# First expert layer as seven products of quarters, read from PSUM between products and interleaved with the second layer

## Chip, cores, metric

The kernel runs on one NeuronCore of a Trainium2 chip. The metric is device time in microseconds (us), the median of several executions. The engines are TensorE (PE in the profile; its weight loads are listed apart as PEld), VectorE (DVE), ScalarE (ACT), GpSimd (POOL) and SyncE (SP). A "call" below is one batch of runs measured together on one chip.

## The reference

An attention block makes a matrix `x` of 4608 tokens by 512; then eight experts, each of two layers, are summed with weights `P` that are balanced by eight rounds of row and column normalisation.

```python
def _moe_ref(x, w_gate, w1, w2):                # x 4608x512, w1 8x512x1024, w2 8x1024x512
    P = exp(logits - max)                       # logits = x @ w_gate, 8 experts
    for _ in range(8):                          # the balancing
        P /= P.sum(1, keepdims=True) + 1e-09
        P /= P.sum(0, keepdims=True) + 1e-09
        P *= N / E
    for e in range(E):
        h = np.maximum(x @ w1[e], 0.0)          # first layer
        out += P[:, e:e+1] * (h @ w2[e])        # second layer
```

## The kernel before

All matmul operands are fp16. `xT` holds x transposed (128 partitions, 4 blocks of the 512 inputs, 4608 tokens). A chunk is 512 tokens. For each chunk the first layer makes 8 hidden tiles of 4 matmuls each, ScalarE applies the relu on the way from PSUM to SBUF, and the second layer makes 4 output tiles of 8 matmuls each, which VectorE scales and adds into `acc`.

```python
def ffn1(hT, w, j, fts=range(FT)):              # FT = 8 hidden tiles
    for ft in fts:
        h_ps = ps_h[ft % len(ps_h)].tile([P, TCH], FP32, name="h_ps")
        for kt in range(KT):                    # KT = 4
            te.matmul(out=h_ps[:], lhsT=w[0][:, kt, ft*P:(ft+1)*P],
                      rhs=xT[:, kt, j*TCH:(j+1)*TCH], start=(kt == 0), stop=(kt == KT-1))
        se.activation(out=hT[:, ft, :], in_=h_ps[:], func=AF.Relu)

def ffn2(hT, e, w, j, ts, y_ps=None, fts=range(FT)):
    # ... 8 matmuls of 512 columns into y_ps, then:
    ve.scalar_tensor_tensor(out=acc(g), in0=y_ps[:], scalar=P_tok[:, g, e:e+1], in1=acc(g),
                            op0=ALU.mult, op1=ALU.add)
    # ... the last expert's rows are stored from here

# attention interleaved with expert 0 on tokens that are ready (cut), then:
for it in range(8): ...                          # balancing: VectorE, with two tiny matmuls a round
for j in range(B, NJ): ffn(0, w0, j)             # rest of expert 0
for g in range(NG): nc.gpsimd.tensor_scalar(...) # acc *= P[:, 0]
for e in range(1, E):
    w = w_next; ...                              # load the next expert's weights
    for j in range(NJ): ffn(e, w, j)
```

The softmax here doesn't subtract the row's maximum and nothing guards it: scores larger than these inputs give would overflow.

## Time and profile before

| before | value | where it stands |
|---|---|---|
| median time | 1101.5 us | runs |
| PE busy | 1074.0 of 1099.8 us | page, part 1 |
| experts 1 to 7, both layers | about 124 us each | 576 matmuls x 215.8 ns |
| PE idle in 185 to 245 us (end of expert 0) | 1.77 us | table by stage, 60.00 - 58.23 |

First the page of the kernel before: the busy times of the engines with instruction counts, and the chain of work that ended last, by engine.

```profile
PE 1074.0 (98%) x6064; PEld 500.9 (46%) x6064; DVE 353.5 (32%) x642; ACT 425.7 (39%) x782; POOL 124.8 (11%) x160
...
PE 92%; DVE 5%; issue 1%; ACT 1%; POOL 1%; DMA 1%; DVEq 0%; POOLq 0%
```

The chain of waits runs through PE for 92% of the span, so PE time is what counts. The groups of instructions (line, engine, operation, output and inputs, count; then busy us, mean ns of one; then idle time before them and what ended it) show where it goes:

```profile
L137 PE MATMUL y_ps<-w2e,hT 128*128 128x512 f16 x2048 | 453.7, 379 | 0.7 <-DVE acc_lo L152 0.7
L122 PE MATMUL h_ps<-xT,w1e 128*128 128x512 f16 x2048 | 454.0, 379 | 0.0
L152 DVE SCALAR_TENSOR_TENSOR acc_lo<-y_ps,P_tok,acc_lo 128x512 f32<-128x512 f32 x224 | 168.3, 751 | 598.4 <-PE y_ps L137 594.3
```

A matmul record lasts 379 ns, but 2048 of them keep PE busy for 454 us, that is 222 ns each: records of consecutive matmuls overlap. The timeline (start, length, engine, operation, count) gives the pitch directly.

```profile
399.66 3.62 PE L137 MATMUL y_ps<-w2e,hT 128*128 128x512 f16 x16
...
400.72 0.75 DVE L152 SCALAR_TENSOR_TENSOR acc_lo<-y_ps,P_tok,acc_lo 128x512 f32<-128x512 f32 x1 [0.98 <-PE y_ps L137]
```

Sixteen matmuls take 3.62 us; without the last one's 0.379 that is 15 pitches of 216 ns. VectorE starts its accumulation at 400.72 while PE goes on. The table by stage (stretch in us, its length, then busy us and count for PE, PEld, DVE, ACT and POOL, then granted clock, DMA share, GB/s) shows the state of the kernel before in its last part:

```profile
185.00:245.00 60.00, 58.23 (x300) 25.72 (x300) 28.70 (x61) 22.87 (x41) 14.28 (x11) 1.00 0.38 61
...
300.00:500.00 200.00, 200.00 (x928) 90.67 (x927) 44.31 (x59) 67.78 (x114) 3.33 (x4) 1.00 0.13 22
```

From 245 us on PE is busy all the time and VectorE is used for 22% (44.31 of 200), ScalarE for 34%. Both have room for extra work, if PE gets less.

### The profile page before, as it was taken

The numbers are of one execution on the slowest core, as the hardware profiler recorded it, in microseconds if no ns is written. First come the engines' busy times: TensorE is split into PE (matmuls) and PEld (weight loads), VectorE is DVE, ScalarE is ACT, GpSimd is POOL, SyncE is SP. The second block draws the span as 40 slices with busy tenths as digits, with TensorE's granted clock in tenths as the row PEclk, the third lists the DMA queues.
The fourth block names the chain that finished last, engine by engine and source line by source line (L and its number), as shares of the span: only waits on it lengthen the run. The fifth ranks groups of instructions, "written<-read, shape, count | busy, mean of one in ns | idle before, by whom it ended". The sixth has DMA issues, their size and how long they took to land.

```text
span 1099.8 us, 14392 instructions
## 1 busy us (share of the span) xinstructions
PE 1074.0 (98%) x6064; PEld 500.9 (46%) x6064; DVE 353.5 (32%) x642; ACT 425.7 (39%) x782; POOL 124.8 (11%) x160
## 2 busy tenths in 40 slices
PE   4899999999999999999999999999999999999998
PEld 3455555444444444444444444444444444444443
DVE  6787775542222222222222222222222222222222
ACT  3666665333333333333333333333333333333332
POOL 7532200059400000000000000000000000000000
PEclk9999999999999999999999999999999999999999
DMA  9965404220004000040004000040004000013333
GB/s 166 195 90 83 66 1 75 42 40 1 1 1 76 1 1 1 1 77 1 1 1 70 8 1 0 1 77 1 1 1 64 14 1 1 1 39 77 77 78 77
DMA packets 34353, 41.32 MB, mean 38 GB/s; under 512 B 3568, under 2 KB 26096, under 8 KB 34288
## 3 DMA queue, kind: packets, MB, share of 16 engines
q0 software_dynamic: 28000, 30.94, 18.2%
q1 hardware_dynamic: 6288, 9.46, 3.8%
q8 instruction: 47, 0.77, 0.3%
q14 instruction: 18, 0.15, 0.0%
HBM read 61.88 MB, written 9.44 MB: 65 GB/s over the span
## 4 chain that ended last, share of the span: by engine, by line
PE 92%; DVE 5%; issue 1%; ACT 1%; POOL 1%; DMA 1%; DVEq 0%; POOLq 0%
PE y_ps L137 40%; PE h_ps L122 39%; PE y_ps L88 5%; PE small_ps L88 4%; PE h_ps L88 4%; DVE k_p L88 1%; DMA k_ld<-in_k_dram 1%; DVE q_p L88 1%; DVE colp L513 0%; DVE v_aug L88 0%; DVE q_pT L88 0%; DVE den L88 0%; DVE P_tok L508 0%; DVE P_tok L523 0%; PE small_ps L519 0%
## 5 line engine op out<-in xcount | busy, mean ns | idle before, releaser
L129 ACT ACTIVATE hT<-h_ps 128x512 f16<-128x512 f32 x512 | 305.7, 597 | 574.7 <-PE h_ps L122 574.7
L137 PE MATMUL y_ps<-w2e,hT 128*128 128x512 f16 x2048 | 453.7, 379 | 0.7 <-DVE acc_lo L152 0.7
L122 PE MATMUL h_ps<-xT,w1e 128*128 128x512 f16 x2048 | 454.0, 379 | 0.0
L152 DVE SCALAR_TENSOR_TENSOR acc_lo<-y_ps,P_tok,acc_lo 128x512 f32<-128x512 f32 x224 | 168.3, 751 | 598.4 <-PE y_ps L137 594.3
L137 PEld LDWEIGHTS <-hT 128*128 128x128 f16 x2048 | 199.9, 98 | 241.2 <-issue 1.0
L122 PEld LDWEIGHTS <-w1e 128*128 128x128 f16 x2048 | 199.7, 98 | 239.7
L103 POOL DMA_DIRECT2D w1e<-in_moe_w_dram x11 | 8.3, 758 | 603.8 <-PE h_ps L122 551.7
L88 PE MATMUL h_ps<-xT,w1e 128*128 128x512 f16 x256 | 65.7, 383 | 0.0
L88 PE MATMUL y_ps<-w2e,hT 128*128 128x512 f16 x256 | 61.4, 380 | 0.0
L542 POOL TENSOR_SCALAR acc_lo<-acc_lo,P_tok 128x512 f32<-128x512 f32 x32 | 49.3, 1556 | 10.1 <-DVE P_tok L523 10.1
L88 ACT ACTIVATE hT<-h_ps 128x512 f16<-128x512 f32 x64 | 38.4, 600 | 21.8 <-PE h_ps L88 21.4
L152 DVE SCALAR_TENSOR_TENSOR acc_hi<-y_ps,P_tok,acc_hi 128x512 f32<-128x512 f32 x28 | 21.0, 751 | 75.7 <-PE y_ps L137 75.7
L88 PE MATMUL small_ps<-ident,q_p 128*128 128x128 f16 x288 | 27.7, 231 | 13.2 <-DVE q_p L88 9.5
L88 PEld LDWEIGHTS <-hT 128*128 128x128 f16 x256 | 22.7, 98 | 29.6 <-issue 6.2
L88 PEld LDWEIGHTS <-q_p 128*128 128x128 f16 x288 | 20.5, 103 | 25.2 <-DVE q_p L88 12.0
L88 ACT COPY rb<-small_ps 128x384 f32<-128x384 f32 x64 | 22.4, 402 | 24.4 <-PE small_ps L88 24.4
L88 DVE TENSOR_TENSOR xT<-small_ps,rb 128x384 f16<-128x384 f32 x64 | 26.3, 453 | 16.9 <-ACT rb L88 15.7
L88 PEld LDWEIGHTS <-w1e 128*128 128x128 f16 x256 | 22.2, 98 | 18.3 <-issue 1.7
L88 DVE TENSOR_SCALAR q_pT<-small_ps 128x384 f16<-128x384 f32 x48 | 26.1, 552 | 6.1 <-PE small_ps L88 5.5
L88 DVE TENSOR_TENSOR k_p<-k_ld,acc_hi 128x1152 f16<-128x1152 f16 x32 | 24.0, 751 | 5.7 <-ACT k_ld L88 5.7
L88 ACT ACTIVATE k_ld<-k_ld 128x576 f16<-128x576 f16 x32 | 22.1, 690 | 6.3 <-DMA k_ld<-in_k_dram 6.3
L88 ACT ACTIVATE q_pT<-small_ps 128x384 f16<-128x384 f32 x48 | 23.6, 497 | 2.3 <-PE small_ps L88 2.3
(80 smaller groups left out, 289.5 us busy)
## 6 DMA issues: line engine op xcount, KB each, us to landing
out_dram<-acc_lo SPq DMA_DIRECT2D x64, 128.0 KB, 2.3
w1e<-in_moe_w_dram POOLq DMA_DIRECT2D x7, 1024.0 KB, 8.2
w2e<-in_moe_w_dram POOLq DMA_DIRECT2D x7, 1024.0 KB, 9.0
q_ld<-in_q_dram POOLq DMA_DIRECT2D x32, 144.0 KB, 4.8
k_ld<-in_k_dram POOLq DMA_DIRECT2D x32, 144.0 KB, 4.6
v_ld<-in_v_dram POOLq DMA_DIRECT2D x32, 144.0 KB, 4.9
w1e<-in_moe_w_dram POOLq DMA_DIRECT2D x4, 256.0 KB, 7.0
w2e<-in_moe_w_dram POOLq DMA_DIRECT2D x4, 256.0 KB, 6.9
```

The source lines that it names most:

```text
L88: return tc.keep_in_program_order(getattr(self.engine, name)(*args, **kwargs))
L103: nc.gpsimd.dma_start(out=w[0][:, :, f0:f1], in_=view[:, :, f0:f1])
L122: te.matmul(out=h_ps[:], lhsT=w[0][:, kt, ft * P : (ft + 1) * P], rhs=xT[:, kt, j * TCH : (j + 1) * TCH], start=(kt == 0), stop=(kt == KT ...
L129: se.activation(out=hT[:, ft, :], in_=h_ps[:], func=AF.Relu)
L137: te.matmul(out=y_ps[:], lhsT=hT[:, ft, ts * P : (ts + 1) * P], rhs=w[1][:, ft, :], start=(ft == 0), stop=(ft == FT - 1),)
L152: ve.scalar_tensor_tensor(out=acc(g), in0=y_ps[:], scalar=P_tok[:, g, e : e + 1], in1=acc(g), op0=ALU.mult, op1=ALU.add,)
L542: nc.gpsimd.tensor_scalar(out=acc(g), in0=acc(g), scalar1=P_tok[:, g, 0:1], scalar2=None, op0=ALU.mult,)
```

## The change

The intent: the first layer of experts 1 to 7 is a matrix product, tokens by hidden units. It is cut into halves of tokens, of inputs and of hidden units, and the eight products of quarters are replaced by seven (Strassen's method in Winograd's form). That takes 7/8 of the columns through PE, and needs sums of quarters of x (once, `S1`, `S2`, `S4`, and one over `a21`), sums of quarters of each expert's weights (`T1` to `T4`), and sums of products. In the code `b11` to `b22` are the quarters of the expert's weights, and `Y` and `Z` are further PSUM banks beside `X`. For the sums of products, partial sums are used twice: a PSUM bank `X` accumulates four products, and ScalarE copies it ("snapshots" `u1`, `u2`, `u4`) between them. PE may write the bank again only after each copy, so second-layer matmuls of the unit before are put in between ("fillers", 4 matmuls each). A unit is 2 x 384 tokens, and has 4 groups; expert 1's first unit carries the end of the balancing in its fillers.

```diff
+    def group(hT, tw, n, i, filler):
+        X = ps_h[0].tile(...); Y = ps_s.tile(...)
+        product(X, b11, x_part(0, 0, n), True)        # each product: 2 matmuls of 384 columns
+        u1 = snapshot(X, "u1")                        # ScalarE copy to fp16
+        product(Y, b21, x_part(0, 1, n), True)
+        add_relu(h11, Y, u1)                          # VectorE: add from PSUM, then max with 0
+        for fn in late: fn()                          # last product of the group before
+        filler()                                      # 4 matmuls of the second layer
+        product(X, T2, s_part(S2, n), False)
+        u2 = snapshot(X, "u2")
+        product(Z, T3, x_part(1, 0, n), True)
+        filler()
+        product(X, T1, s_part(S1, n), False)
+        u4 = snapshot(X, "u4")
+        add_relu(h22, Z, u4)
+        filler()
+        product(X, b22, s_part(S4, n), False)
+        nc.scalar.activation(out=h12, in_=X[:, 0:TU], func=AF.Relu)
+        def last():
+            product(Z, T4, x_part(1, 1, n), False)
+            add_relu(h21, Z, u2)
+        late.append(last)
 ...
-    for e in range(1, E):
-        for j in range(NJ):
-            ffn(e, w, j)
+    for e in range(1, E):
+        for n in range(NU):                           # 6 units
+            if e == 1 and n == 0: ... tws[i] = w_sums(w, i)       # sums of weights
+            if e == 1 and n + 2 < NU: for _ in x_sums(n + 2): pass # sums of x
+            for i in range(FH):                       # 4 groups
+                group(hT, tws[i], n, i, fill)
+                ...                                   # weight sums for the next expert
+            pending = halves(...)                     # this unit's second layer, in fillers of the next
```

Four more parts came with it. PE's instructions are now in written order for the whole kernel (before, a scheduler placed them after the attention). The balancing is spread over the end of expert 0 and the first unit of expert 1. The tile `hA`, expert 0's hidden tile of the attention part, now shares memory with what follows. The very last store is issued by ScalarE. A few buffer counts changed with it (`hB` from 3 to 2, the small PSUM tiles from 2 to 4).

Copying a bank in the middle of its accumulation rests on what the Trainium skill says in "PSUM — Partial Sum Buffer", "The four PSUM rules": only the first-matmul flag clears anything, and a matmul without it adds to what the bank holds; the last-matmul flag has no effect.

More of the change, by code (lines that the diff above doesn't have):

```diff
@@ L59 @@
     wA = ctx.enter_context(tc.tile_pool(name="wA", bufs=1))
-    hA = ctx.enter_context(tc.tile_pool(name="hA", bufs=1))
     sk_pool = ctx.enter_context(tc.tile_pool(name="sk_pool", bufs=2))
@@ L84, in __init__ @@
             self.engine = engine
+            self.last = None
         def __getattr__(self, name):
             def call(*args, **kwargs):
-                return tc.keep_in_program_order(getattr(self.engine, name)(*args, **kwargs))
+                i = getattr(self.engine, name)(*args, **kwargs)
+                if self.last is not None:
+                    tc.add_manual_dep(
+                        i.ins,
+                        self.last.ins.name,
+                        mybir.DependencyInfo(
+                            mybir.DependencyClass.NoSync, mybir.DependencyReason.DATA
+                        ),
+                        reason="written order",
+                    )
+                self.last = i
+                return i
             return call
@@ L128, in ffn1, with ffn2 @@
                 )
-            se.activation(out=hT[:, ft, :], in_=h_ps[:], func=AF.Relu)
-    def ffn2(hT, e, w, j, ts, y_ps=None, fts=range(FT)):
-        g = j * TCH // P + ts
+            se.activation(out=hT[:, ft, 0:TCH], in_=h_ps[:], func=AF.Relu)
+    def ffn2(hT, e, w, c0, g, y_ps=None, fts=range(FT)):
         if y_ps is None:
@@ L138, in ffn2 @@
                 out=y_ps[:],
-                lhsT=hT[:, ft, ts * P : (ts + 1) * P],
+                lhsT=hT[:, ft, c0 : c0 + P],
                 rhs=w[1][:, ft, :],
@@ L160, in ffn2 @@
                     rows = out[b * S : (b + 1) * S].rearrange("(p c) d -> p c d", c=C)
-                    nc.sync.dma_start(
+                    (nc.scalar if half and g == NG - 1 else nc.sync).dma_start(
                         out=rows[:, c, :], in_=acc(g)[half * HP : (half + 1) * HP, :]
@@ L165 @@
     with ExitStack() as p1:
+        hA = p1.enter_context(tc.tile_pool(name="hA", bufs=1))
         cs_pool = p1.enter_context(tc.tile_pool(name="cs_pool", bufs=1))
@@ L483 @@
                     at(j, NS - 1, turn, b + 1, hk, k_)
-        for j in range(B):
+        for j in range(B - 1):
             hT = hA.tile([P, FT, TCH], F16, name="hT")
@@ L492 @@
                         y_ps = ps_y.tile([P, Dm], FP32, name="y_ps")
-                    ffn2(hT, 0, w0, j, ts, y_ps, range(part * FT // 2, (part + 1) * FT // 2))
+                    ffn2(
+                        hT, 0, w0, ts * P, j * TCH // P + ts, y_ps,
+                        range(part * FT // 2, (part + 1) * FT // 2),
+                    )
                 for fn, args in todo.get((j, slot), []):
                     fn(*args)
-    te, ve, se = free
-    ps_h.append(ctx.enter_context(tc.tile_pool(name="ps_h2", bufs=2, space=bass.MemoryType.PSUM)))
@@ L500 @@
-    ps_s = ctx.enter_context(tc.tile_pool(name="ps_k", bufs=2, space=bass.MemoryType.PSUM))
-    for it in range(8):
-        rs = sk_pool.tile([P, NG], FP32, name="rs")
-        nc.vector.reduce_sum(out=rs[:], in_=P_tok[:], axis=AX.X)
-        rr = sk_pool.tile([P, NG], FP32, name="rr")
-        nc.vector.reciprocal(out=rr[:], in_=rs[:])
-        nc.vector.tensor_tensor(
-            out=P_tok[:], in0=P_tok[:],
-            in1=rr[:].unsqueeze(2).to_broadcast([P, NG, E]), op=ALU.mult,
-        )
-        colp = sk_pool.tile([P, E], FP32, name="colp")
-        nc.vector.reduce_sum(out=colp[:], in_=P_tok[:].rearrange("p c e -> p e c"), axis=AX.X)
-        tot_ps = ps_s.tile([P, 512], FP32, name="small_ps")
-        nc.tensor.matmul(out=tot_ps[0:1, 0:E], lhsT=ones_col[:], rhs=colp[:], start=True, stop=True)
-        t2 = sk_pool.tile([1, E], FP32, name="t2")
-        nc.vector.reciprocal(out=t2[:], in_=tot_ps[0:1, 0:E])
-        bc_ps = ps_s.tile([P, 512], FP32, name="small_ps")
-        nc.tensor.matmul(
-            out=bc_ps[:, 0:E], lhsT=scale_row[0:1, 1 if it == 7 else 0, :], rhs=t2[0:1, :],
-            start=True, stop=True,
-        )
-        nc.vector.tensor_tensor(
-            out=P_tok[:], in0=P_tok[:],
-            in1=bc_ps[:, 0:E].unsqueeze(1).to_broadcast([P, NG, E]), op=ALU.mult,
-        )
@@ L528 @@
-    wB = ctx.enter_context(tc.tile_pool(name="wB", bufs=1))
-    hB = ctx.enter_context(tc.tile_pool(name="hB", bufs=3))
-    w_next = load_weights(wB, 1)
-    def ffn(e, w, j):
-        hT = hB.tile([P, FT, TCH], F16, name="hT")
-        ffn1(hT, w, j)
-        for ts in range(TCH // P):
-            ffn2(hT, e, w, j, ts)
-    for j in range(B, NJ):
-        ffn(0, w0, j)
-    for g in range(NG):
-        nc.gpsimd.tensor_scalar(
-            out=acc(g), in0=acc(g), scalar1=P_tok[:, g, 0:1], scalar2=None, op0=ALU.mult,
-        )
+    ve, se = nc.vector, nc.scalar
@@ new lines @@
+    ps_s = ctx.enter_context(tc.tile_pool(name="ps_k", bufs=4, space=bass.MemoryType.PSUM))
+    wB = ctx.enter_context(tc.tile_pool(name="wB", bufs=1))
+    hB = ctx.enter_context(tc.tile_pool(name="hB", bufs=2))
+    s_pool = ctx.enter_context(tc.tile_pool(name="s_pool", bufs=1))
+    t_pool = ctx.enter_context(tc.tile_pool(name="t_pool", bufs=1))
+    u_pool = ctx.enter_context(tc.tile_pool(name="u_pool", bufs=2))
+    NT = N // 2
+    TU = 3 * P
+    NU = NT // TU
+    KH = KT // 2
+    FH = FT // 2
@@ new lines, with x_part, s_part, x_sums @@
+    UG = TU // P
+    w_next = load_weights(wB, 1)
+    S1, S2, S4 = (s_pool.tile([P, KH, NT], F16, name=name) for name in ("S1", "S2", "S4"))
+    def x_part(half, kh, n):
+        t0 = half * NT + n * TU
+        return xT[:, kh * KH : (kh + 1) * KH, t0 : t0 + TU]
+    def s_part(t, n):
+        return t[:, :, n * TU : (n + 1) * TU]
+    def x_sums(n):
+        a11, a12, a21, a22 = (x_part(i, j, n) for i in range(2) for j in range(2))
+        s1, s2, s4 = (s_part(t, n) for t in (S1, S2, S4))
+        for out_, in0, in1, op in (
+            (s1, a21, a22, ALU.add), (s2, s1, a11, ALU.subtract),
+            (s4, a12, s2, ALU.subtract), (a21, a11, a21, ALU.subtract),
+        ):
+            nc.vector.tensor_tensor(out=out_, in0=in0, in1=in1, op=op)
+            yield
@@ new lines, in w_sums @@
+    def w_sums(w, i):
+        cols = [slice((j * FH + i) * P, (j * FH + i + 1) * P) for j in range(2)]
+        b11, b12 = (w[0][:, 0:KH, c] for c in cols)
+        b21, b22 = (w[0][:, KH:KT, c] for c in cols)
+        T2, T3, T4 = (t_pool.tile([P, KH, P], F16, name=f"T{k_}_{i}") for k_ in (2, 3, 4))
+        nc.vector.tensor_tensor(out=T3[:], in0=b22, in1=b12, op=ALU.subtract)
+        nc.vector.tensor_tensor(out=T2[:], in0=T3[:], in1=b11, op=ALU.add)
+        nc.vector.tensor_tensor(out=T4[:], in0=b21, in1=T2[:], op=ALU.subtract)
+        nc.vector.tensor_tensor(out=b12, in0=b12, in1=b11, op=ALU.subtract)
+        return b11, b12, b21, b22, T2[:], T3[:], T4[:]
@@ new lines, in product, with add_relu, snapshot @@
+    def product(ps, lhs, rhs, start):
+        for kh in range(KH):
+            te.matmul(
+                out=ps[:, 0:TU], lhsT=lhs[:, kh, :], rhs=rhs[:, kh, :],
+                start=(start and kh == 0), stop=(kh == KH - 1), skip_group_check=True,
+            )
+    def add_relu(out, ps, t):
+        nc.vector.tensor_tensor(out=out, in0=ps[:, 0:TU], in1=t[:], op=ALU.add)
+        nc.vector.tensor_scalar(out=out, in0=out, scalar1=0.0, scalar2=None, op0=ALU.max)
+    def snapshot(ps, name):
+        t = u_pool.tile([P, TU], F16, name=name)
+        nc.scalar.copy(out=t[:], in_=ps[:, 0:TU])
+        return t
@@ new lines @@
+    late = []
+    def group(hT, tw, n, i, filler):
+        b11, T1, b21, b22, T2, T3, T4 = tw
+        h11, h12 = hT[:, i, 0:TU], hT[:, FH + i, 0:TU]
+        h21, h22 = hT[:, i, TU : 2 * TU], hT[:, FH + i, TU : 2 * TU]
+        X = ps_h[0].tile([P, TCH], FP32, name="h_ps")
+        Y = ps_s.tile([P, 512], FP32, name="small_ps")
+        product(X, b11, x_part(0, 0, n), True)
+        u1 = snapshot(X, "u1")
+        product(Y, b21, x_part(0, 1, n), True)
+        add_relu(h11, Y, u1)
+        for fn in late:
+            fn()
+        late.clear()
+        filler()
+        Z = ps_s.tile([P, 512], FP32, name="small_ps")
+        product(X, T2, s_part(S2, n), False)
[12 more added lines that the diff above has]
+        late.append(last)
@@ new lines, in sinkhorn @@
+    def sinkhorn():
+        for it in range(8):
+            rs = sk_pool.tile([P, NG], FP32, name="rs")
+            nc.vector.reduce_sum(out=rs[:], in_=P_tok[:], axis=AX.X)
+            rr = sk_pool.tile([P, NG], FP32, name="rr")
+            nc.vector.reciprocal(out=rr[:], in_=rs[:])
+            nc.vector.tensor_tensor(
+                out=P_tok[:], in0=P_tok[:],
+                in1=rr[:].unsqueeze(2).to_broadcast([P, NG, E]), op=ALU.mult,
+            )
+            colp = sk_pool.tile([P, E], FP32, name="colp")
+            nc.vector.reduce_sum(
+                out=colp[:], in_=P_tok[:].rearrange("p c e -> p e c"), axis=AX.X
+            )
+            tot_ps = ps_s.tile([P, 512], FP32, name="small_ps")
+            te.matmul(out=tot_ps[0:1, 0:E], lhsT=ones_col[:], rhs=colp[:], start=True, stop=True)
+            t2 = sk_pool.tile([1, E], FP32, name="t2")
+            nc.vector.reciprocal(out=t2[:], in_=tot_ps[0:1, 0:E])
+            yield
+            bc_ps = ps_s.tile([P, 512], FP32, name="small_ps")
+            te.matmul(
+                out=bc_ps[:, 0:E], lhsT=scale_row[0:1, 1 if it == 7 else 0, :], rhs=t2[0:1, :],
+                start=True, stop=True,
+            )
+            nc.vector.tensor_tensor(
+                out=P_tok[:], in0=P_tok[:],
+                in1=bc_ps[:, 0:E].unsqueeze(1).to_broadcast([P, NG, E]), op=ALU.mult,
+            )
+            yield
@@ new lines, in halves, with gate @@
+    def halves(hT, e, w, tiles):
+        for c0, g in tiles:
+            y_ps = ps_y.tile([P, Dm], FP32, name="y_ps")
+            for part in range(2):
+                ffn2(hT, e, w, c0, g, y_ps, range(part * FT // 2, (part + 1) * FT // 2))
+                yield
+    gate_order = [half * (NG // 2) + n * UG + i for n in range(NU) for half in range(2) for i in range(UG)]
+    def gate(tiles):
+        for g in tiles:
+            nc.gpsimd.tensor_scalar(
+                out=acc(g), in0=acc(g), scalar1=P_tok[:, g, 0:1], scalar2=None, op0=ALU.mult,
+            )
@@ new lines @@
+    balance = sinkhorn()
+    sums_x = (None for n in range(2) for _ in x_sums(n))
+    for j in range(B - 1, NJ):
+        hT = hB.tile([P, FT, 2 * TU], F16, name="hT")
+        tiles = halves(hT, 0, w0, [(ts * P, j * TCH // P + ts) for ts in range(TCH // P)])
+        for slot in range(NS):
+            if slot < FT:
+                ffn1(hT, w0, j, [slot])
+            elif j < NJ - 1:
+                next(tiles)
+            else:
+                break
+            if j == B - 1 and slot == 0:
+                gates(B - 1)
+            if j == NJ - 1:
+                next(sums_x)
+            if ((j - B + 1) * NS + slot) % 5 < 2 and (j > B - 1 or slot >= 5):
+                next(balance)
@@ L545, with fill @@
+    pending = tiles
+    tws = [None] * FH
+    k_fill = 0
+    def fill():
+        nonlocal k_fill
+        first = k_fill < 3 * FH
+        if not first or k_fill % 3 < 2:
+            next(pending, None)
+        if first and k_fill % 3 > 0:
+            next(balance)
+        k_fill += 1
     for e in range(1, E):
         w = w_next
-        if e + 1 < E:
-            w_next = load_weights(wA if e % 2 else wB, e + 1)
-        for j in range(NJ):
-            ffn(e, w, j)
+        for n in range(NU):
+            hT = hB.tile([P, FT, 2 * TU], F16, name="hT")
+            if e == 1:
+                if n == 0:
+                    for i in range(FH):
+                        tws[i] = w_sums(w, i)
+                if n + 2 < NU:
+                    for _ in x_sums(n + 2):
+                        pass
+                if n:
+                    gate(gate_order[(n - 1) * 2 * UG : n * 2 * UG])
+            elif e == 2 and n == 0:
+                gate(gate_order[(NU - 1) * 2 * UG :])
+            for i in range(FH):
+                group(hT, tws[i], n, i, fill)
+                if e > 1 and n == 0 and i == 0:
+                    tws[FH - 1] = w_sums(w, FH - 1)
+                if e + 1 < E and n == NU - 1 and i:
+                    tws[i - 1] = w_sums(w_next, i - 1)
+            for _ in pending:
+                pass
+            if n == 0 and e + 1 < E:
+                w_next = load_weights(wA if e % 2 else wB, e + 1)
+            pending = halves(
+                hT, e, w,
+                [(h * TU + i * P, h * (NG // 2) + n * UG + i) for h in range(2) for i in range(UG)],
+            )
@@ L553 @@
+    for fn in late:
+        fn()
+    for _ in pending:
+        pass
 _INS = ['q', 'k', 'v', 'moe_w_gate', 'moe_w1', 'moe_w2']
```

## The prediction

> What bounds the kernel now: TensorE. The page gives PE 98% busy (1074 of 1099.8 us) and the chain of waits is 92% PE. From about 240 us (experts 1 to 7) the table by stage shows PE busy 100 of every 100 us, clock 1.00, VectorE 21 to 23%, ScalarE 33 to 36%. In the timeline 16 back-to-back 512-column matmuls span 3.62 us including a last one of 0.379, a pitch of 216 ns, weight loads (98 ns) hidden. This agrees with the Trainium skill, "TensorE: Matmul & The Clock Gate", "Wait — 56ns, not 53.3ns?": columns/2.4 GHz + 2.5 ns = 215.8 ns.
>
> Removed: in experts 1 to 7, first layer, 288 matmuls of 512 columns per expert: 7 x 288 x 215.8 = 435.1 us. Added: 336 matmuls of 384 columns per expert. By the same formula 162.5 ns (estimate with that page's 2.5 ns; no run here shows it yet): 7 x 336 x 162.5 = 382.2 us. Gain on the critical path 52.9 us, so 1048.6 us with no new wait.
>
> Per group (14 product matmuls, three fillers of 4 second-layer matmuls, 4.86 us of PE):
> - ScalarE: three snapshots and one relu of 128x384, about 0.49 us each (trace: 479 to 497 ns): 2.0 us.
> - VectorE: three adds from PSUM (trace: 558 ns for such a 128x384), three maxima (estimate 0.25 us), 1.5 accumulations of 0.751: 3.55 us, 73%, against 21% now. Latency now matters.
> Waits: the tightest is the u4 snapshot: result 0.16 us after the product's slot, 0.04 to start (trace: VectorE 40 ns after the modelled end), 0.49 copy, 0.06 back (trace: PE after VectorE), so about 0.76 us against a filler of 0.86: just hidden. The second accumulator (Z) must be read before T4, with some 0.5 us to spare; weight sums (16 x about 0.28 us per expert) sit before it at an expert's end: 0.5 us lost per expert, 3 us in all.
>
> Transition (end of expert 0, first unit of expert 1): here VectorE gets 23 sums of 768 elements (about 0.55 us, scaled from 750 ns for 1152), 16 weight sums (4.5 us) and the balancing (8 x 2.6 us) in one FIFO. Up to the first product that is about 32 us of VectorE against 24 us of PE, and PE waits in written order for each balancing step. I expect 10 to 15 us of new PE waits between about 190 and 240 us, less about 2 us idle there before.
>
> Risk: during expert 1 GpSimd scales 36 tiles (1.56 us each) while VectorE runs maxima. The skill, "SBUF — State Buffer", has the shared port pair as an exclusive lock; no run here shows it. 0 to 10 us; I allow 2.
>
> Sum: 1048.6 + 11 + 3 + 2 = about 1064 us. 8 in 10: 1051 to 1082. Chances: faster by over 2% 0.90, within 2% 0.085, slower 0.015.
>
> What would show it: pitch of 384-column matmuls about 162 ns; steady stages (experts 2 to 7) 117 us per expert instead of 124, PE 98% or more; VectorE about 70 to 75% there, ScalarE about 40%; PE waits for balancing tiles and S sums concentrated at 190 to 240 us; PE<-ScalarE (u4) waits below 0.1 us per group.
>
> What would make it wrong: snapshots slower than estimated (0.1 us late per group is 17 us over 168 groups); weight loads not hidden under 160 ns; VectorE maxima blocked by GpSimd; VectorE delaying Z in every group; the transition stalling over 20 us; a lowered clock.

## The result, and the profile after

The changed kernel took 1053.42 us (1052.66 to 1054.63, 4 runs) against 1101.51: ratio 0.9564, 95% interval 0.9547 to 0.958. The outputs are right. A ratio here is the mean time of one kernel's fast runs over that of the other's of the same rounds, so it is not quite the ratio of the medians quoted. The prediction was 1064, range 1051 to 1082: the direction and the range held, and the gain was larger than the middle of the forecast (48.1 us, not 37.5).

The page of the changed kernel, the same two lines as before:

```profile
PE 1021.2 (97%) x6400; PEld 533.9 (51%) x6400; DVE 738.9 (70%) x1786; ACT 429.7 (41%) x950; POOL 125.2 (12%) x160
...
PE 91%; DVE 5%; DMA 1%; ACT 1%; issue 1%; POOL 0%; POOLq 0%; DVEq 0%; ACTq 0%
```

PE is 97% busy, and still 91% of the chain. VectorE rose from 32 to 70%. By stage:

```profile
185.00:245.00 60.00, 53.66 (x296) 25.82 (x294) 48.85 (x131) 23.18 (x47) 10.40 (x9) 1.00 0.45 71
245.00:300.00 55.00, 55.00 (x295) 28.75 (x294) 43.03 (x84) 20.46 (x45) 48.67 (x32) 1.00 0.00 1
300.00:500.00 200.00, 199.96 (x1070) 104.45 (x1068) 137.71 (x340) 74.46 (x164) 3.33 (x4) 1.00 0.14 22
```

In the last of the three stretches PE executes 1070 matmuls instead of 928, since most of them are shorter. One group in the timeline, from its b22 product to the next one; lines on `h_ps<-S_...` are products on bank X, `u_...` the snapshots:

```profile
499.77 0.49 PE L88 MATMUL h_ps<-S_3370,w1e 128*128 128x384 f16 x2
...
503.45 0.49 PE L88 MATMUL h_ps<-S_3368,w1e 128*128 128x384 f16 x2
...
503.78 1.03 PE L88 MATMUL y_ps<-w2e,hT 128*128 128x512 f16 x4
504.03 0.48 ACT L577 CAST u_6433<-h_ps 128x384 f16<-128x384 f32 x1 [1.05 <-PE h_ps L88]
...
504.64 0.49 PE L88 MATMUL h_ps<-S_3370,w1e 128*128 128x384 f16 x2
```

The b22 products start at 499.77 and 504.64: a group takes 4.87 us (4.86 was predicted). Twelve filler matmuls at 215.8 ns are 2.59 us, so the 14 products' matmuls have a pitch of (4.87 - 2.59) / 14 = 163 ns, which agrees with the 162.5 of the prediction. The tight place is also here: the T1 product starts at 503.45, its snapshot runs from 504.03 for 0.48 us, and b22 on the same bank starts at 504.64, 0.13 us after the snapshot's end.

What PE waited for from 186 to 250 us (what waited, for whom: us in total, times, longest):

```profile
PE small_ps L88 <- DVE colp L628: 2.7, 5, 1.4
PE small_ps L88 <- DVE t_3439 L634: 2.7, 1, 2.7
PE h_ps L88 <- ACT u_3776 L577: 0.3, 1, 0.3
PE h_ps L88 <- ACT u_3668 L577: 0.3, 1, 0.3
```

No PE wait at all is listed after 250 us. So the give-back is at the end of expert 0 alone. PE's idle time in 185 to 245 us is 60.00 - 53.66 = 6.34 us, against 1.77 before.

### The profile page after: what moved, and what is told of

Its sections match the earlier page's. It is cut to its first block, busy times and chain, and to the rows that moved or that the text cites. A ratio compares the mean times of both kernels' runs of the same rounds, so it can differ in the third digit from the quotient of the medians.

```text
span 1051.0 us, 16774 instructions
## 1 busy us (share of the span) xinstructions
PE 1021.2 (97%) x6400; PEld 533.9 (51%) x6400; DVE 738.9 (70%) x1786; ACT 429.7 (41%) x950; POOL 125.2 (12%) x160
## 4 chain that ended last, share of the span: by engine, by line
PE 91%; DVE 5%; DMA 1%; ACT 1%; issue 1%; POOL 0%; POOLq 0%; DVEq 0%; ACTq 0%
PE y_ps L88 47%; PE h_ps L88 24%; PE small_ps L88 20%; DVE k_p L88 1%; DMA w1e<-in_moe_w_dram 1%; DMA k_ld<-in_k_dram 1%; DVE q_p L88 0%; DVE v_aug L88 0%; DVE q_pT L88 0%; DVE den L88 0%; DVE colp L628 0%; DVE hT L572 0%; ACT k_ld L88 0%; ACT kv_sb L88 0%; ACT hT L88 0%
## 5 line engine op out<-in xcount | busy, mean ns | idle before, releaser
L88 PE MATMUL y_ps<-w2e,hT 128*128 128x512 f16 x2304 | 585.5, 379 | 0.0
L88 PEld LDWEIGHTS <-w1e 128*128 128x128 f16 x1632 | 155.9, 98 | 143.2 <-issue 2.8
L88 PE MATMUL h_ps<-xT,w1e 128*128 128x384 f16 (+1 forms) x624 | 155.4, 352 | 0.0
L607 ACT ACTIVATE hT<-h_ps 128x384 f16<-128x384 f32 x168 | 82.4, 490 | 109.6 <-PE h_ps L88 109.6
L573 DVE TENSOR_SCALAR hT<-hT 128x384 f16<-128x384 f16 x504 | 123.7, 273 | 2.9
L88 PE MATMUL h_ps<-S_3370,w1e 128*128 128x384 f16 x336 | 82.1, 326 | 0.9 <-ACT u_3776 L577 0.3
L88 PE MATMUL h_ps<-S_3368,w1e 128*128 128x384 f16 x336 | 82.1, 326 | 0.0
L88 PE MATMUL small_ps<-xT,w1e 128*128 128x384 f16 x336 | 82.1, 326 | 0.0
L88 ACT ACTIVATE hT<-h_ps 128x512 f16<-128x512 f32 x56 | 33.6, 600 | 17.9 <-PE h_ps L88 17.5
L88 ACT ACTIVATE q_pT<-small_ps 128x384 f16<-128x384 f32 x48 | 23.7, 498 | 2.5 <-PE small_ps L88 2.5
```

The costliest lines, as they stand in the source:

```text
L88: i = getattr(self.engine, name)(*args, **kwargs)
L573: nc.vector.tensor_scalar(out=out, in0=out, scalar1=0.0, scalar2=None, op0=ALU.max)
L607: nc.scalar.activation(out=h12, in_=X[:, 0:TU], func=AF.Relu)
```

## The experiments

### e1_eight: the same order with eight products

```diff
-  seven products, snapshots, add_relu
+  for each quarter of h: product(X, l0, r0, True); product(X, l1, r1, False)
+      nc.scalar.activation(out=quarter, in_=X[:, 0:TU], func=AF.Relu); filler()
-  sums of x and of the weights
```

> Same written order, same fillers, same 384-column units, but the first layer of experts 1 to 7 as 8 ordinary products of quarters (16 matmuls a group instead of 14), no sums, no snapshots, one ScalarE relu per quarter. Theory (the gain is the eighth of the streamed columns): 7 x 24 groups x 2 more matmuls x 162.5 ns = +54.6 us over the changed kernel's 1053.4, less up to 4.5 us of PE waits at the end of expert 0 that the sums cause: 1103 to 1108 us, no faster than before (1101.5). Rival (the gain comes from the interleaving and the written order on PE): well under 1090 us.

Measured: 1100.07 us (1099.49 to 1100.7), ratio to before 0.9986, interval 0.9971 to 1.0001. The line by stage for the end of expert 0:

```profile
185.00:245.00 60.00, 59.81 (x332) 29.18 (x333) 27.89 (x60) 25.82 (x52) 16.04 (x13) 1.00 0.45 71
```

Interleaving, written order and the smaller units bring almost nothing by themselves; the gain of the change is the eighth of the columns. The time is 3 us below the expected span. About half of that is in this line: PE idle is 0.19 us, so the sums had cost 6.15 us of PE waits in the changed kernel and not the 4.5 that I subtracted. (The remainder of under 2 us is no larger than the scatter between calls that shows up below; it was not explained further.)

### e2_blocks: no second layer between the products

```diff
-                group(hT, tws[i], n, i, fill)
+                group(hT, tws[i], n, i, fill if e == 1 and n == 0 else lambda: None)
```

> The seven products kept, but the second layer taken out from between them: from the second unit of expert 1 on, the four groups of a unit run without fillers, then the six output tiles of the unit before. Theory (each snapshot's copy and its two handovers, about 0.75 us from the product's slot to the next product on the same bank, is covered only by the fillers): waits of about 0.2 us before T2, 0.4 before T1, 0.75 before b22, so 1.35 us a group, 164 groups: about +220 us, near 1275 us, slower than the kernel before. Rival ([...]the other products cover the copies anyway): within 10 us of 1053.

Measured: 1279.59 us, one run (its state is unknown, but 226 us is far outside any state's effect here). The PE waits after 245 us:

```profile
PE h_ps L88 <- ACT u L577: 149.0, 327, 0.9
```

Without fillers the seven products are 16% slower than eight ordinary ones. The list shows only 149 us of the loss: a wait that is shorter than the modelled tail of a matmul record is hidden by that tail, and of a longer one a part. (A 384-column record lasts 0.326 us by the groups of instructions of the changed kernel, at a pitch of 0.163. In a group of e2_blocks at 501 us, PE stood for 0.13 us before T2, which is not listed, 0.45 before T1, listed as 0.29, and 0.77 before b22, listed as 0.62. So some 0.46 us a group is hidden, 75 us in 164 groups, and 226 - 149 is 77.) The interleaving is what makes the method pay, and 0.75 us per handover was the right size.

### e3_third3 and e4_third5: one matmul moved between fillers

```diff
-            next(pending, None)              # half a tile: 4 matmuls
+            for _ in range((4, 5, 3)[k_fill % 3]):   # e4: (4, 3, 5); the first unit of expert 1 keeps 4
+                next(pending, None)          # one matmul each
```

> Fillers of 4, 5 and 3 matmuls instead of 4, 4, 4 from the second unit of expert 1 on; the same work, only the last filler (between the T1 product with its u4 snapshot and the b22 product) is 216 ns shorter and the middle one longer. In the trace of the changed kernel u4 ends at 504.51 us and b22 starts at 504.64; with a 60 ns handover the slack is 0.07 us. Theory (that chain is the tightest of the steady stage and just hidden): 0.216 - 0.07 = 0.146 us lost a group, 164 groups: +24 us, about 1077 us. Rival (there is more slack than the records show): under +5 us.

> Fillers of 4, 3 and 5: the last one 216 ns longer, the middle one (before T1, after the u2 snapshot) shorter. In the trace u2 ends at 502.99 and T1 starts at 503.45, slack about 0.4 us, so 0.22 us can go. Theory (the steady stage is bound by the PE alone, no wait left to remove): no change, within 1 us of 1053.4. Rival (the thin u4 slack costs something that the records hide): some us faster.

Measured: e3 1077.62 us (1077.08 to 1078.24), e4 1055.33 us (1054.75 to 1055.72). The lines by stage, e3 first, then e4:

```profile
300.00:500.00 200.00, 199.75 (x1040) 101.39 (x1040) 134.30 (x332) 72.54 (x160) 3.33 (x4) 1.00 0.14 22
```

```profile
300.00:500.00 200.00, 200.00 (x1070) 104.58 (x1069) 137.37 (x340) 74.59 (x165) 3.33 (x4) 1.00 0.14 22
```

e3 is 22.3 us slower than e4 and 24.2 slower than the changed kernel's first measurement; the forecast was 24. In e3 the snapshot and the next product stand like this:

```profile
504.09 0.49 PE L88 MATMUL h_ps<-S,w1e 128*128 128x384 f16 x2
...
504.67 0.48 ACT L577 CAST u<-h_ps 128x384 f16<-128x384 f32 x1 [1.26 <-PE h_ps L88]
...
505.20 0.48 PE L88 MATMUL h_ps<-S,w1e 128*128 128x384 f16 x2
```

The snapshot ends at 504.67 + 0.48 = 505.15 and b22 starts at 505.20: a handover of 0.05 us, with nothing to spare. So the last filler of 4 matmuls covers the copy with about 0.07 us left over, and one matmul fewer in each group costs half of what the whole change had gained. e4 shows that there is nothing left to win by a longer one: 1070 matmuls in 200 us, as in the changed kernel. Its 1055.3 us lie outside "within 1 us of 1053.4", but inside what the changed kernel itself gave when repeated (a0_again), so no difference is shown.

The e3 line also holds a warning. PE is listed as busy for 199.75 of 200 us, yet does 1040 matmuls instead of 1070. The loss of about 0.14 us a group (22.3 us in 164 groups, against e4) is almost invisible in busy time. The Trainium skill says so in its first page, "Trainium Kernel Development and Optimization", "Best Practices": matmul busy time is a bad measure of how close PE is to its limit. The count of matmuls in a stretch showed the loss.

### a0_again, e5a_load, e7_defer, e8_both: the end of expert 0

In the changed kernel the longest PE wait of that stage is 2.67 us, for `t_3439`, the reciprocal in the first balancing round. VectorE's timeline shows why: the operation ahead of it is a sum of expert 1's weights, which have not arrived.

```profile
189.02 0.55 DVE L548 TENSOR_TENSOR S_3369<-S_3368,xT 128x768 f16<-128x768 f16 x1
189.48 0.55 DVE L548 TENSOR_TENSOR xT<-xT 128x768 f16<-128x768 f16 x1
189.95 0.45 DVE L620 TENSOR_REDUCE rs<-P_tok 128x36 f32<-128x288 f32 x1
...
193.36 0.56 DVE L548 TENSOR_TENSOR xT<-xT 128x768 f16<-128x768 f16 x1
197.13 0.29 DVE L557 TENSOR_TENSOR T_0_3597<-w1e 128x256 f16<-128x256 f16 x1 [3.22 <-DMA w1e<-in_moe_w_dram]
197.34 0.19 DVE L634 RECIPROCAL t_3439<-small_ps 1x8 f32<-1x8 f32 x1
```

The first three lines also show how VectorE runs: operations of 0.55 us that do not depend on the one just before start 0.46 to 0.47 us apart. The last two show the queue: `T_0` waits until 197.13 for the transfer, and the reciprocal behind it can only follow. The transfer started late, at 188.77 us (before: at 180.02), because its buffer lies in memory that the attention stage used to its end: `hA` shares it, which PE read until about 188 us, and the profile names VectorE's last attention product (`xT`, until 188.5) as what released it. Which of the two decided was not separated.

```diff
 e5a_load
+    hB = ctx.enter_context(tc.tile_pool(name="hB", bufs=2))
     wB = ctx.enter_context(tc.tile_pool(name="wB", bufs=1))
-    hB = ctx.enter_context(tc.tile_pool(name="hB", bufs=2))
 e7_defer, in addition: the sums of x for unit n + 1 are written after the first group of unit n
 (n = 1 to 4), and tied behind the last add of that group so that they are not scheduled earlier
 e8_both: as e7_defer, but wB is the last pool opened, so that S1, S2, S4 lie in memory that is free early
```

> The changed kernel unaltered, as the control of this chip and call: 1053.4 us within 1.5, with the 2.7 us PE wait for the balancing step behind the first weight sum, and in some executions a PE clock below 1 for some microseconds after that wait (seen in the profiles of two runs of the first call, not in the first profile of the changed kernel).

> Only the order of two buffer pools is swapped, so that the weights of expert 1 no longer lie where the last hidden tile of expert 0's first part lay, and their transfer can start some 10 us earlier. Theory (late weights block the VectorE queue, in which the first weight sum stands before the reciprocal that the PE waits for): the 2.67 us wait goes, and with it the dip of the PE clock behind it: 2.7 to 4 us faster than the control, about 1050 us. Rival (VectorE is the limit there anyway, so the wait moves to the next balancing steps): under 1 us faster.

> As e5a_load, and the sums of x for units 2 to 5 are held back to the unit before their use (16 VectorE operations leave the end of expert 0). Theory (the other PE waits at the end of expert 0, 1.36 and 0.39 us for column sums, are VectorE's queue): another 1.5 to 2.5 us, about 1048 us; in units 1 to 4 VectorE has room (4 x 0.47 us more in 19.5 us) and PE waits stay 0. Rival (the balancing's own chain of dependent operations sets the pace, or the held sums delay the Z adds later): no gain over e5a_load, or new PE waits in units 1 to 4.

> As e7_defer, but with the buffers placed so that also the S sums of units 0 and 1 can run before the attention ends. Theory (VectorE still has room there): equal to e7_defer or up to 1 us faster, near 1047 us, which is the changed kernel without its 6.2 us of extra PE idle time between 185 and 245 us (6.34 against 0.19 in the kernel of eight products). Rival (the early sums stand in VectorE's queue before the last attention block's denominators, on which the PE waits): slower than e7_defer by up to 2 us.

| kernel | median us | range | ratio to before | PE idle 185 to 245 us |
|---|---|---|---|---|
| a0_again | 1055.63 | 1054.66 to 1056.66 | 0.9586 | 6.49 |
| e5a_load | 1049.86 | 1049.45 to 1050.43 | 0.9534 | 3.66 |
| e7_defer | 1048.06 | 1047.29 to 1048.53 | 0.9517 | 1.91 |
| e8_both | 1054.73 | 1054.52 to 1056.18 | 0.958 | 5.18 |

The start of the first weight transfer of expert 1 in a0_again, in e5a_load and in e8_both (the last number of each line is the idle time of POOL before it, and what ended it):

```profile
189.57 0.75 POOL L114 DMA_DIRECT2D w1e<-in_moe_w_dram  x1 [60.55 <-DVE xT L88]
```

```profile
173.97 0.75 POOL L114 DMA_DIRECT2D w1e<-in_moe_w_dram  x1 [45.18 <-ACT kv_sb L88]
```

```profile
190.43 0.75 POOL L114 DMA_DIRECT2D w1e<-in_moe_w_dram  x1 [61.50 <-DVE xT L88]
```

And the stage in e5a_load and in e7_defer:

```profile
185.00:245.00 60.00, 56.34 (x311) 27.19 (x308) 49.88 (x133) 24.30 (x50) 10.95 (x8) 1.00 0.27 43
```

```profile
185.00:245.00 60.00, 58.09 (x320) 28.29 (x319) 48.12 (x125) 24.85 (x51) 13.37 (x10) 1.00 0.26 42
```

e5a_load moves the transfer forward by 15.6 us, and gains 5.8 us over its control, more than the 2.7 to 4 expected. The difference is the PE clock. In the control's profile the 2.84 us wait is followed by matmuls at half pace:

```profile
198.55 0.59 PE L88 MATMUL small_ps<-t,scale_row 1*128 1x8 f32 x2 [2.84 <-DVE t L634]
199.07 1.89 PE L88 MATMUL h_ps<-xT,w1e 128*128 128x512 f16 x4
200.75 4.79 PE L88 MATMUL y_ps<-w2e,hT 128*128 128x512 f16 x12
```

In the first profile of the changed kernel, with a wait of 2.67 us, they were not:

```profile
197.90 1.04 PE L88 MATMUL h_ps<-xT,w1e 128*128 128x512 f16 x4
198.78 2.75 PE L88 MATMUL y_ps<-w2e,hT 128*128 128x512 f16 x12
```

Four matmuls take 1.89 us instead of 1.04, twelve take 4.79 instead of 2.75, and the two small ones 0.59 instead of 0.38 (in the other profile): together 3.1 us. The granted clock over 185 to 215 us is 0.89 in the control and 1.00 in e5a_load. The profiles of e3 and e4 had this dip too, and a shorter one stands in e2_blocks (1.7 us lost). So one late transfer costs 2.7 us in some executions and up to about 6 in others. That is enough to explain that the changed kernel measured 1053.4 in one call and 1055.6 in another; it is not shown, since each call has the profile of one execution (the two profiled executions are 4.0 us apart, of which the dip is 3.1). The Trainium skill describes such a throttle in "TensorE: Matmul & The Clock Gate", "HAM oscillation — how this bites in real kernels", with idle gaps over about 3.4 us as the condition, and says under "What's actually happening" that the window is free-running; here a listed wait of 2.7 to 2.8 us was enough in some executions.

e7_defer gains another 1.8 us (1.5 to 2.5 expected): with 16 VectorE operations out of the way, the waits of 1.36 and 0.39 us for column sums are gone. No PE wait appeared in units 1 to 4.

e8_both missed: it was expected at 1047 and took 1054.7. Half of the rival was right: the early sums stood in front of the last attention block's denominators, on which PE waited 1.2 us more. The larger part is a cost that I had not expected. With the pools in that order the weights lie in memory that VectorE's last attention product (`xT`) frees, so the transfer starts at 190.43 and the old wait is back (last line below). The clock dip is back too: it starts about 1 us after that wait, and twelve matmuls take 4.44 us instead of 2.75, another 1.7 us that I had overlooked.

```profile
201.42 4.44 PE L88 MATMUL y_ps<-w2e,hT 128*128 128x512 f16 x12
...
PE small_ps L88 <- DVE hl L88: 4.1, 3, 2.6
PE small_ps L88 <- DVE t L643: 3.3, 1, 3.3
```

### e7_again, e9_max2, e10_store: room on VectorE, and the last store

```diff
 e9_max2, on e7_defer
+        for _ in range(2):
             nc.vector.tensor_scalar(out=out, in0=out, scalar1=0.0, scalar2=None, op0=ALU.max)
 e10_store, on e7_defer
-                    (nc.scalar if half and g == NG - 1 else nc.sync).dma_start(
+                    nc.sync.dma_start(
```

> The best kernel so far again, as the control of this call: 1048.1 us within 1.

> As e7_defer, but every maximum on VectorE is done twice (three more operations of 0.25 us a group, which change no value). Theory (VectorE at about 69% has room, and only the Z add has a deadline, some 0.5 us away): VectorE rises to about 85%, PE waits stay near 0 except beside the weight sums at an expert's end: at most +6 us over the control. Rival (with 70% busy, VectorE's queue already decides when Z and the hidden tiles are ready): 0.3 us or more a group, +50 us.

> As e7_defer, but the very last store is issued by SyncE again, as in the kernel before, instead of by ScalarE. Theory: the two last stores are issued one after the other, some 0.6 us of issue each, so at most 0.7 us slower than the control. Rival: no difference that the runs can show.

Measured: e7_again 1047.82 us (ratio 0.9515, interval 0.9502 to 0.9528), e9_max2 1053.49, e10_store 1048.79 (interval 0.9506 to 0.9532). For e9_max2, the steady stage and the PE waits after 210 us:

```profile
300.00:500.00 200.00, 200.00 (x1071) 104.53 (x1069) 161.92 (x469) 74.80 (x165) 3.33 (x4) 1.00 0.14 22
```

```profile
PE small_ps L88 <- DVE hT L580: 3.7, 3, 1.3
PE small_ps L88 <- DVE colp L638: 2.2, 3, 1.0
PE h_ps L88 <- ACT u L586: 1.0, 4, 0.3
```

With VectorE at 81% (161.92 of 200) PE still does 1071 matmuls in 200 us, so in the steady stage VectorE's queue has room: the theory holds there. The 5.7 us lost are all before 300 us: 2.2 us for column sums and 1.0 for snapshots before 245 us (0.9 and 0.6 in the control), and 3.7 us for `hT` adds between 245 and 300 us (none in the control), where GpSimd scales its 36 tiles. The weight sums at the experts' ends, which I had named as the place, cost nothing even then.

e10_store is 1.0 us slower by the medians, but the intervals overlap, so by the times whether ScalarE's store matters stays open. The two profiles point to the theory: from the start of the last accumulation to the end of the span, 4.4 us pass in e7_again (1041.82 to 1046.2) and 5.0 us in e10_store (1042.28 to 1047.3).

e7_defer is the fastest kernel: 5% faster than before.

## Why the prediction was right, and where it was off

- **What bounds the kernel, and the gain.** "Gain on the critical path 52.9 us": right. The pitch of the 384-column matmuls is 163 ns (predicted 162.5), a group takes 4.87 us (predicted 4.86), and e1_eight, which gives the eighth back, is 52.0 us slower than e7_defer, which has lost nearly all the new waits (1100.07 against 1048.06, from different calls). With 384-column matmuls the eighth is 54.6 us, and e7_defer has 1.7 us more PE idle than e1_eight (1.91 - 0.19), so 52.9 would be expected there too.
- **Snapshots.** "just hidden", 0.76 us against 0.86: right, and shown by e3_third3, where 0.216 us less cover cost 24 us, and by e2_blocks, where no cover cost 226 us.
- **The end of expert 0.** "10 to 15 us of new PE waits", less 2: too large. The trace has 6.34 us of PE idle against 1.77 before, 4.6 more. The step that failed is "about 32 us of VectorE against 24 us of PE". I added up record lengths. The same operations, from the first row sum at 189.95 to the first add at 217.66, took 27.7 us, of which 4.0 were idle: 23.7 us of work, about as much as PE did there (23.3 us busy). The Trainium skill has the reason in "Perfetto Trace Analysis", "Optimizing Scalar/DVE Operations": part of a record's length, the write acknowledgement, overlaps with the next instruction. Here 0.55 us records start 0.47 us apart, so of the 8 us too much some 5 come from 66 operations counted 0.07 to 0.08 us too long each (their records add up to 28.6 us). The rest is mostly the balancing: 32 us, less the sums, leaves 14.9 us for it, and the rounds that fell into the stretch add up to 11.5 us. The groups of the kernel before did not show the overlap, because accumulations that stand alone have a busy time of count times mean (224 x 751 ns = 168.3 us); the timeline of before did, where a VectorE operation of 0.75 us that starts at 167.24 is followed by another at 167.90.
- **What I missed there.** The largest single wait, 2.67 us, was not VectorE's amount of work, but one operation in its queue that waited for a transfer, and e5a_load removes it. Of the predicted kind, balancing steps that wait in VectorE's queue, the list has only the 2.7 us for `colp`. The clock dip that follows in some executions (3.1 us) was only in my list of dangers, with another cause.
- **Weight sums at an expert's end**, "3 us in all": the trace shows no PE wait after 250 us, so 0.
- **GpSimd and the maxima**, "0 to 10 us; I allow 2": the effect exists, and costs PE nothing. The maxima while GpSimd scales its tiles, and after (count: shortest, median, longest ns):

```profile
L573 DVE TENSOR_SCALAR hT<-hT x28: 246/526/982, 247.6 to 290.9; 128x384 f16<-128x384 f16 x28
```

```profile
L573 DVE TENSOR_SCALAR hT<-hT x30: 249/252/262, 300.6 to 346.6; 128x384 f16<-128x384 f16 x30
```

While GpSimd works, their median is 526 ns and the longest 982, against 252 after it, as the exclusive port pair of the skill's page (its section "Who interferes with whom") leads one to expect. VectorE's adds from PSUM keep their 0.54 to 0.56 us in both stretches, so not all of VectorE is slowed. PE, however, is busy for all of 245 to 300 us, presumably since nothing that PE waits for soon depends on a maximum. That the port is the cause was not isolated by an experiment; only the coincidence is shown. e9_max2 shows that the stretch is sensitive: doubling the maxima cost 3.7 us there.

In sum: of 52.9 us expected from PE, 4.6 were given back at the end of expert 0, 48.3 remain, and 48.1 was measured. All three amounts that the prediction subtracted (11, 3 and 2 us) were too large, so the time lies near the lower end of the stated range; that it was not further off owes something to chance, since more than half of the 4.6 us is a wait that the prediction did not have.

## What to carry to other kernels

A method with fewer multiplications adds reads of PSUM between its products; on this PE-bound kernel it paid only where other matmuls covered every such read. Count the handover (slot of the product, copy, start of the next) against the filler, since one matmul too few per group ate half of the gain. Put nothing into a queue that waits for a transfer ahead of something short that PE needs, and look at which freed buffer a prefetch has to wait for: swapping two allocations was worth 5.8 us here. When costing a busy queue, use the distance between starts of consecutive records, not their lengths, and judge PE by matmuls per stretch, not by busy time.

## What the Trainium skill lacked or had wrong

- "TensorE: Matmul & The Clock Gate" gives idle gaps over about 3.4 us as what throttles PE. Here listed waits of 2.7 to 2.8 us did it in some executions and not in others: matmuls at half pace for some 6 us, 3.1 us lost. (Counted from the end of the last matmul's slot, the gaps were 2.9 to 3.0 us in the control, e3 and e4, and 2.85 in the first profile of the changed kernel, which has no dip. The table in the page's section "Why this matters for your kernels" gives about 3 us, which is closer.)
- "VectorE: DVE Perf Modes", "The DRAIN you can't avoid", says that the next operation does not start until the pipe is empty, and refers elsewhere for the exceptions. Here independent operations of 550 ns start 467 ns apart. A number for the cost of an operation after overlap is not lacking: it stands in "Vector Engine (DVE) Microarchitecture Reference", "5.2 Measured stream behaviour on trn2", and looked up in time it would have avoided my error.
- No page has the length of the whole handover from a PSUM bank through a ScalarE copy and back to PE. In these traces, for 384 columns: 0.25 us from the end of the product's slot (503.78) to the start of the copy (504.03), 0.48 us of copy, and, in e3_third3 where PE waits for it, 0.05 us to the next product.
- "Trainium Kernel Development and Optimization" warns that matmul busy time misleads, but not that the list of waits does too: in e2_blocks 149 us of waits were listed for a loss of 226 us, and in e3_third3 next to none for 24 us.
